# Capped attention and two feed-forward blocks: attention as one phase, two batches per pass over the weights

## The chip, the cores and the metric

The kernel runs on one core of a Trainium2 chip. The metric is the device time of one execution in microseconds. A core has TensorE (matmuls; PE, its weight loads PEld), VectorE (DVE), ScalarE (ACT), GpSimd (POOL) and SyncE (SP), whose queue issues all DMAs here.

## The reference

```python
# q, k, v: (4 batches, 12 heads, 448, 64) float32; weights arrive as float64
scores = cap * tanh(q @ k.T / 8 / cap)                  # per batch and head
attn = exp(scores - max); attn /= sum(attn)
x = (attn @ v), heads side by side                      # 1792 x 768
h = x @ w_in;  x = (h - tanh(h)) @ w_out                # 768 x 2048, 2048 x 768
h = x @ w_in2; out = (h * sigmoid(1.702 * h)) @ w_out2  # same sizes
```

## The kernel before

All activations lie with features on partitions and the 448 tokens of a batch as columns. A batch has six pairs of heads for attention, then four products (input and output of two layers), each 96 products of 128 x 128 weights by 448 columns.

**Attention of a pair** g: `prep` transposes q and k (TensorE) and copies them from PSUM; `pair_scores` makes scores for two of four key blocks; `tanh` and `exps` run on ScalarE over 112 x 896; `add` sums the exponentials on VectorE; `pair_pv` multiplies by v; `pair_sum` sums over keys with a matmul by ones; `pair_out` takes the reciprocal and the product. In the first batch (g < 6) this is float32 and runs alone, in an order written out by hand in `attention` (pinned by `pin`). The pairs of batches 1 to 3 are steps of a generator that the main loop at the end takes between feed-forward matmuls, at rates given by `ATT_RATES`; their scores are three float32r products of high and low halves.

**Weights** come in pieces ("chunks") of up to 6 x 128 x 128. `w_convert` makes float32 from the float64 words in four steps on ScalarE and VectorE (exponent, low bits, shift, or) and stores the result in DRAM (`kept`). Batch 0 uses the float32 piece as it is, with whole float32 matmuls. From batch 1 on `w_split` makes a float32r high half (`hi_act`, L95) and a low half (`lo_dve`, L101), for each batch anew, but for the first 16 pieces, whose halves are kept too. The products are then high x high, high x low, low x high.

**Between the products** `g_cubic` (layer one) makes h - tanh(h) with four ScalarE and four VectorE operations per 448 columns, L506 to L525; `g_gate` (layer two) takes one of each. From batch 1 on `g_split` adds a high half (ScalarE and VectorE in turn) and a low half on GpSimd (L104). The last product's columns are tokens; `final` transposes them back on TensorE ahead of the store.

**Order.** Tile's planner orders what is not pinned, by its own costs, within what buffers allow. `ahead` prepares pieces 4 (first batch) or 2 ahead; there are three buffers each for the double-width, float32 and half pieces.

Of the kernel before, what the change touches and what calls it, by code (L numbers as in the profile page):

```python
# [29 lines left out]
ATT_RATES = {"first": (0.0, 0.7, 0.7, 1.3), "last": (0.3, 1.1, 0.7, 1.1), "mid": (0.3, 0.9, 0.9, 0.8)}  # L30
ATT_END_0, ATT_END = 1.0, 0.97

LATE_AT = 8

LEAD_0 = 4
# [5 lines left out]
def attention_moe_moe(ctx, tc, q, k, v, cap, w_in1, w_out1, w_in2, w_out2, out):  # L41

# [9 lines left out]
    WCH = 6  # L66
# [6 lines left out]
    raw_p = pool("raw", 1)  # L73
    rv_p = pool("rawv", 2)
    st_p = pool("stk", 2)
    t_p = pool("t", 6)
    ts_p = pool("tsum", 2)
    w_p = pool("w", 2)
    big = pool("big", 1)
    g_p = pool("g", 2)  # L80
    g1_p = pool("g1", 1)
    wd_p = pool("wdbl", 3)
    wr_p = pool("wraw", 3)
# [3 lines left out]
    ps_b = pool("ps_b", 2, space=bass.MemoryType.PSUM)  # L87
# [12 lines left out]
    def lo_dve(dst, src, hi):  # L100
        nc.vector.tensor_tensor(out=dst, in0=src, in1=hi.bitcast(F32), op=ALU.subtract)  # L101

    def lo_pool(dst, src, hi):
        nc.gpsimd.tensor_tensor(out=dst, in0=src, in1=hi.bitcast(F32), op=ALU.subtract)  # L104
# [11 lines left out]
    xs_p = pool("xs", 2)  # L116
    xd = [dr_p.tile([P, S], F32, name=f"xd{i}") for i in range(NP)]
    xst = {}
    xf = [big.tile([P, S], F32, tag=f"xh{i}", name=f"xf{i}") for i in range(KM)]
    xh = [None] * KM  # L120
    xl = [big.tile([P, S], F32R, name=f"xl{i}") for i in range(KM)]

    first = ExitStack()
    t_f = first.enter_context(tc.tile_pool(name="t_f", bufs=4))
    wz_f = first.enter_context(tc.tile_pool(name="wz_f", bufs=1))
    raw_f = first.enter_context(tc.tile_pool(name="raw_f", bufs=2))
    ps_f = first.enter_context(tc.tile_pool(name="ps_f", bufs=2, space=bass.MemoryType.PSUM))
# [4 lines left out]
    for wi, wo in ((w_in1, w_out1), (w_in2, w_out2)):  # L132
        wi, wo = wi.bitcast(U32), wo.bitcast(U32)
        for f in range(KF):
            chunks.append((wi[:, 2 * f * P:2 * (f + 1) * P], 0, KM))
        for e in range(KM):
            for f0, f1 in parts:
                chunks.append((wo[:, 2 * e * P:2 * (e + 1) * P], f0, f1))
    NCH = len(chunks)
    split_kept = [i < KF for i in range(NCH)]  # L140
    kept_hl = [
        dr_p.tile([P, 2, k1 - k0, P], F32, name=f"kept_hl{i}") if split_kept[i] else None
        for i, (_, k0, k1) in enumerate(chunks)
    ]
    kept = [dr_p.tile([P, k1 - k0, P], F32, name=f"kept{i}") for i, (_, k0, k1) in enumerate(chunks)]
    dbls, raws, whl = {}, {}, {}
    gf, gh, gl = [None] * KF, [None] * KF, []
    n_dma, n_split, n_use = [0], [0], [0]

    n_dbl = [0]  # L150

    def dbl_dma():
        if n_dbl[0] < NCH:
            i = n_dbl[0]
            src, k0, k1 = chunks[i]
            t = wd_p.tile([P, WCH, P, 2], U32, tag="wd", name="wd")
            for a in range(k0, k1, WG):
                z = min(k1, a + WG)
                nc.sync.dma_start(
                    out=t[:, a - k0:z - k0].rearrange("p k f w -> p k (f w)"),  # L160
                    in_=src[a * P:z * P].rearrange("(k p) f -> p k f", p=P),
                )
            dbls[i] = t[:, :k1 - k0]
            n_dbl[0] += 1

    def w_dma(upto):
        while n_dma[0] <= min(upto, B * NCH - 1):
            i = n_dma[0]
            _, k0, k1 = chunks[i % NCH]
            if i >= 2 * NCH and split_kept[i % NCH]:  # L170
                h = wh_p.tile([P, WCH, P], F32R, tag="wh", name="wh")
                l = wh_p.tile([P, WCH, P], F32R, tag="wl", name="wl")
                for m, t in enumerate((h, l)):
                    nc.sync.dma_start(out=t[:, :k1 - k0].bitcast(F32), in_=kept_hl[i % NCH][:, m])
                whl[i] = (h, l)
            elif i >= NCH:
                t = wr_p.tile([P, WCH, P], F32, tag="wr", name="wr")
                nc.sync.dma_start(out=t[:, :k1 - k0], in_=kept[i % NCH])
                raws[i] = t
            n_dma[0] += 1  # L180

    def w_convert(i):
        _, k0, k1 = chunks[i]
        if i % 2:
            r = wh_p.tile([P, WCH, P], F32, tag="wh", name="wr")
        else:
            r = wr_p.tile([P, WCH, P], F32, tag="wr", name="wr")
        d = dbls.pop(i)
        high, half = d[:, :, :, 1], d.bitcast(U16)
        o = r[:, :k1 - k0]  # L190
        u = o.bitcast(U32)
        pin(nc.scalar.mul(out=o, in_=high.bitcast(F32), mul=2.0 ** -112))
        if i % 2:
            pin(nc.vector.tensor_scalar(
                out=half[:, :, :, 2], in0=half[:, :, :, 1], scalar1=F64_LOW, scalar2=None, op0=ALU.mult
            ))
        else:
            pin(nc.scalar.mul(out=half[:, :, :, 2], in_=half[:, :, :, 1], mul=F64_LOW))
        pin(nc.vector.tensor_scalar(out=u, in0=u, scalar1=3, scalar2=None, op0=ALU.logical_shift_left))
        pin(nc.vector.scalar_tensor_tensor(  # L200
            out=u, in0=high, scalar=0x80000007, in1=u, op0=ALU.bitwise_and, op1=ALU.bitwise_or
        ))
        dbl_dma()
        nc.sync.dma_start(out=kept[i], in_=r[:, :k1 - k0])
        return r

    def w_split(upto):
        while n_split[0] <= min(upto, B * NCH - 1):
            i = n_split[0]
            if i in whl:  # L210
                n_split[0] += 1
                continue
            _, k0, k1 = chunks[i % NCH]
            n = k1 - k0
            r = w_convert(i) if i < NCH else raws.pop(i)
            if i < NCH:
                whl[i] = (r, None)
                n_split[0] += 1
                continue
            h = wh_p.tile([P, WCH, P], F32R, tag="wh", name="wh")  # L220
            l = wh_p.tile([P, WCH, P], F32R, tag="wl", name="wl")
            hi_act(h[:, :n], r[:, :n])
            lo_dve(l[:, :n], r[:, :n], h[:, :n])
            if i // NCH == 1 and split_kept[i % NCH]:
                for m, t in enumerate((h, l)):
                    nc.sync.dma_start(out=kept_hl[i % NCH][:, m], in_=t[:, :n].bitcast(F32))
            whl[i] = (h, l)
            n_split[0] += 1

    def w_next():  # L230
        i = n_use[0]
        n_use[0] += 1
        w_split(i)
        return i, whl.pop(i)
# [4 lines left out]
    tt, sc_t, ts_t, r_t, sum_t = {}, {}, {}, {}, {}  # L239
    raw_done = set()  # L240
    last_raw = [None]

    def load_qk(g):
        if g >= NG or g in raw_done:
            return
        raw_done.add(g)
        b, hp = divmod(g, NP)
        t = (raw_f if g < NP and g % 3 else raw_p).tile([CP, 2, 2 * C * D], F32, tag="raw", name="raw")
# [8 lines left out]
    def load_v(g):  # L257
        if g >= NG or g in rawv:
            return
# [8 lines left out]
    def prep(g, i):  # L268
        t = raw[g]
        if i == 0:  # L270
            if g < NP:
                qkt[g] = st_p.tile([P, 2, S], F32, tag="ql", name="qk")
            else:
                qkt[g] = tuple(st_p.tile([P, 2, S], F32R, tag=tag, name=name) for tag, name in (("qh", "qk"), ("ql", "ql")))
        else:
            raw.pop(g)
        if 1 < g < NP:
# [5 lines left out]
        if g < NP:  # L283
            (hi_act if g == 0 and i else hi_dve)(qkt[g][:, i], ps[:, :S])
            return
        h, l = qkt[g]
        hi_act(h[:, i], ps[:, :S])
        lo_dve(l[:, i], ps[:, :S], h[:, i])

    def pair_kq(g, c):  # L290

        ps = ps_b.tile([CP, 2, 512], F32, tag="b", name="ps_sc")
        if g >= NP:
            h, l = qkt[g]
            seq = ((h, h), (h, l), (l, h))
        else:
            seq = ((qkt[g], qkt[g]),)
        for m, (qq, kk) in enumerate(seq):
            for j in range(2):
                a = slice(j * D, (j + 1) * D)  # L300
                pin(nc.tensor.matmul(  # L301
                    ps[:, j, :S], kk[a, 1, c * CP:(c + 1) * CP], qq[a, 0],
                    start=(m == 0), stop=(m == len(seq) - 1),
                ))
        sc_t[g, c] = ps

    def tanh(g, c):
        t = tt[g, c] = (t_f if g < NP and c % 2 else t_p).tile([CP, 2, S], F32, tag="t", name="t")
        pin(nc.scalar.activation(out=t, in_=sc_t.pop((g, c))[:, :, :S], func=AF.Tanh, scale=tsc[:CP]))  # L309

    def exps(g, c):

        t = tt[g, c]
        pin(nc.scalar.activation(out=t, in_=t, func=AF.Exp, scale=cpos[:CP]))  # L314
# [397 lines left out]
```

## Time and profile before

| | |
|---|---|
| three runs | 1227.54, 1227.92, 1228.9 us; median 1227.92 |
| profiled execution | 1227.54 us; its span 1225.8 us |
| TensorE busy | 1206.6 us, 98% |
| VectorE, ScalarE, GpSimd busy | 732.0, 696.7, 120.9 us |
| granted TensorE clock, mean | 0.997 |
| DMA | 202.86 MB, 165 GB/s in the mean |

The span runs from the first to the last instruction. Busy times are unions over an engine's instructions; a line such as L558 is a line of the kernel, and a helper's line (L95, L101) holds many uses of it.

### The profile page before, as it was taken

To read this page: it belongs to the slowest core of one execution; us is meant where nothing else is said; L and a number is where in the kernel's file an instruction comes from. 1 tells how busy PE (TensorE), PEld (TensorE's weight loads), DVE (VectorE), ACT (ScalarE), POOL (GpSimd) and SP (SyncE) were. 2 spreads that over 40 slices of the span, in tenths; PEclk is the share of its full clock that TensorE was granted. 3 is DMA by queue.
4 is the path that set the end of the run, shared out by engine and by line. 5 is a ranking of instruction groups with operands and counts; after the bars stand their busy time and mean duration, and the time that the engine had idled before them with its cause. 6 is when DMAs were issued, how large, how long until landed. Compare 5 with 4: busy or idle time off the path is not lost.

```text
span 1225.8 us, 15375 instructions
## 1 busy us (share of the span) xinstructions
PE 1206.6 (98%) x5535; PEld 895.7 (73%) x5535; DVE 732.0 (60%) x946; ACT 696.7 (57%) x953; POOL 120.9 (10%) x102
## 2 busy tenths in 40 slices
PE   9899999999999999999999999999999999999998
PEld 3245555545455788887788899887988799999997
DVE  5989845666554898455553589445455478534432
ACT  7889746566664677456654367556455467334421
POOL 0000000000000132002210033001310023103300
PEclk9999999999999999999999999999999999999999
DMA  8369887966765575343334575343443376333342
GB/s 205 108 219 313 278 259 240 294 216 216 240 196 164 207 271 163 113 120 96 115 107 141 166 211 152 104 120 115 114 123 115 106 225 175 109 119 107 96 126 57
DMA packets 163675, 202.86 MB, mean 165 GB/s; under 512 B 53264, under 2 KB 120592, under 8 KB 163600
## 3 DMA queue, kind: packets, MB, share of 16 engines
q1 hardware_dynamic: 163600, 201.89, 53.9%
q8 instruction: 43, 0.70, 0.2%
q14 instruction: 32, 0.26, 0.1%
HBM read 156.76 MB, written 45.09 MB: 165 GB/s over the span
## 4 chain that ended last, share of the span: by engine, by line
PE 88%; ACT 5%; DVE 4%; issue 1%; DMA 1%; SPq 0%; DVEq 0%; ACTq 0%
PE ps_y L582 39%; PE ps_h L558 39%; PE ps_sc L301 3%; PE ps_pv L332 3%; ACT t L309 2%; ACT t L314 2%; PE ps_r L345 1%; PE ps_qk L282 1%; DVE w L357 1%; PE ps_o L607 1%; DVE ts L324 1%; DMA raw<-in_k_dram 0%; DVE wl L101 0%; DVE ts L322 0%; PE wps L635 0%
## 5 line engine op out<-in xcount | busy, mean ns | idle before, releaser
L101 DVE TENSOR_TENSOR wl<-wr,wh 128x768 fp32r<-128x768 f32 (+1 forms) x172 | 159.9, 932 | 206.8 <-PE ps_y L582 88.0
L95 ACT CAST wh<-wr 128x768 fp32r<-128x768 f32 (+1 forms) x172 | 135.3, 788 | 210.8 <-PE ps_y L582 163.8
L558 PE MATMUL ps_h<-xh,wh 128*128 128x448 f32 x576 | 213.1, 370 | 3.9 <-DVE g_far L507 3.0
L582 PE MATMUL ps_y<-gl,wh 128*128 128x448 f32 x576 | 213.0, 370 | 0.0
L558 PE MATMUL ps_h<-xl,wh 128*128 128x448 f32 x576 | 212.2, 368 | 0.0
L582 PE MATMUL ps_y<-g,wh 128*128 128x448 f32 x576 | 210.9, 366 | 0.0
L582 PE MATMUL ps_y<-g,wr 128*128 128x448 f32 x384 | 148.1, 541 | 0.0
L558 PE MATMUL ps_h<-xf,wr 128*128 128x448 f32 x384 | 146.3, 540 | 0.5 <-DVE xf L353 0.5
L582 PE MATMUL ps_y<-g,wl 128*128 128x448 f32 x576 | 136.8, 367 | 0.0
L558 PE MATMUL ps_h<-xh,wl 128*128 128x448 f32 x576 | 133.8, 366 | 0.0
L104 POOL TENSOR_TENSOR gl<-g_q,g 128x448 fp32r<-128x448 f32 x48 | 63.4, 1321 | 702.8 <-ACT g L95 600.3
L558 PEld LDWEIGHTS ps_h<-xf,wr 128*128 128x128 f32 x384 | 72.2, 190 | 71.1 <-issue 69.3
L558 PEld LDWEIGHTS ps_h<-xh,wh 128*128 128x128 f32 x576 | 108.8, 189 | 15.9 <-DVE g_far L507 4.3
L582 PEld LDWEIGHTS ps_y<-g,wr 128*128 128x128 f32 x384 | 71.6, 190 | 66.7 <-issue 66.3
L309 ACT ACTIVATE t<-ps_sc,tsc 112x896 f32<-112x896 f32 x96 | 94.8, 1000 | 42.5 <-PE ps_sc L301 42.4
L558 PEld LDWEIGHTS ps_h<-xl,wh 128*128 128x128 f32 x576 | 108.9, 189 | 10.3 <-issue 0.8
L582 PEld LDWEIGHTS ps_y<-gl,wh 128*128 128x128 f32 x576 | 108.2, 188 | 11.0 <-issue 2.0
L582 PEld LDWEIGHTS ps_y<-g,wl 128*128 128x128 f32 x576 | 107.4, 188 | 10.7 <-issue 2.3
L558 PEld LDWEIGHTS ps_h<-xh,wl 128*128 128x128 f32 x576 | 108.0, 188 | 9.4 <-issue 0.3
L582 PEld LDWEIGHTS ps_y<-g,wh 128*128 128x128 f32 x576 | 108.3, 188 | 8.7 <-issue 0.3
L314 ACT ACTIVATE t<-t,cpos 112x896 f32<-112x896 f32 x96 | 98.8, 1043 | 1.9
L104 POOL TENSOR_TENSOR gl<-g_g,g 128x448 fp32r<-128x448 f32 x48 | 56.7, 1184 | 337.7 <-ACT g L95 247.5
(73 smaller groups left out, 1382.4 us busy)
## 6 DMA issues: line engine op xcount, KB each, us to landing
wr<-kept SPq DMA_DIRECT2D x100, 384.0 KB, 3.0
wd<-in_moe_w_in_dram SPq DMA_DIRECT2D x64, 384.0 KB, 4.8
wr<-kept SPq DMA_DIRECT2D x72, 320.0 KB, 2.9
wd<-in_moe_w_out_dram SPq DMA_DIRECT2D x48, 384.0 KB, 4.7
kept<-wr SPq DMA_DIRECT2D x44, 384.0 KB, 5.4
wh<-kept_hl SPq DMA_DIRECT2D x32, 384.0 KB, 3.4
wl<-kept_hl SPq DMA_DIRECT2D x32, 384.0 KB, 3.8
kept<-wr SPq DMA_DIRECT2D x24, 320.0 KB, 5.0
```

The lines of the kernel that those rows point to most:

```text
L95: pin(nc.scalar.copy(out=dst, in_=src))
L101: nc.vector.tensor_tensor(out=dst, in0=src, in1=hi.bitcast(F32), op=ALU.subtract)
L104: nc.gpsimd.tensor_tensor(out=dst, in0=src, in1=hi.bitcast(F32), op=ALU.subtract)
L282: pin(nc.tensor.transpose(ps[:, c * CP:(c + 1) * CP], t[:, i, c * P:(c + 1) * P], ident[:CP, :CP]))
L301: pin(nc.tensor.matmul(ps[:, j, :S], kk[a, 1, c * CP:(c + 1) * CP], qq[a, 0], start=(m == 0), stop=(m == len(seq) - 1),))
L309: pin(nc.scalar.activation(out=t, in_=sc_t.pop((g, c))[:, :, :S], func=AF.Tanh, scale=tsc[:CP]))
L314: pin(nc.scalar.activation(out=t, in_=t, func=AF.Exp, scale=cpos[:CP]))
L324: pin(nc.vector.tensor_tensor(out=ts_t[g], in0=ts_t[g], in1=t, op=ALU.add))
L332: pin(nc.tensor.matmul(r_t[g][j * D:(j + 1) * D, :S], rawv[g][:, j, kc, :], t[:, j], start=(kc == 0), stop=(kc == C - 1),))
L345: pin(nc.tensor.matmul(sum_t[g][j * D:(j + 1) * D, :S], ones[:CP], of[:, j], start=first, stop=last))
L558: pin(nc.tensor.matmul(ps[:, :S], w[:, kk, :], x[kk], start=(m == 0), stop=(m == len(seq) - 1)))
L582: nc.tensor.matmul(ps[:, :S], w[:, f - f0, :], x[f], start=(c == 0 and m == 0), stop=(c == len(parts) - 1 and m == len(seq) - 1),)
```

## The change

- Attention of all four batches is one phase ahead of the feed-forward, in the pinned order that only the first batch had, in float32 throughout. x of batches 0 and 1 is split into halves inside that phase (one tile in every second pair); x of batches 2 and 3 is stored to DRAM (`x_store`) and read back in the second pass (`x_next`). Two pieces of weights are converted and split in the phase, a step per pair.
- The feed-forward runs in two passes over the weights; each piece serves two batches in turn. All four batches use three float32r products. In the first pass every piece is converted, split and stored as halves (ScalarE: exponent, every other time the low bits, high half; VectorE: shift, or, low half, the low bits of the others); the second pass loads halves only. `LEAD` is 2; double-width and float32 pieces have two buffers, halves three.
- The low half of g is made on VectorE; g's high half on ScalarE.
- The last product has 128 tokens of the two batches as weights and 384 columns of w_out2 as moving operand, so that PSUM holds rows of tokens: seven banks at a time, twice per pass. `rows_out` scales them by 0.5 into one of two buffers and stores them in two DMAs; the transposes at the end are gone.
- PSUM in the feed-forward is eight single banks.

The diff, cut to its core:

```diff
+    wd_p = pool("wdbl", 2)
+    wr_p = pool("wraw", 2)
     wh_p = pool("whl", 3)
...
+            for half in range(2):
+                for f in range(0, KF, 2):
+                    chunks.append((wo[:, 2 * half * HW:2 * (half + 1) * HW], f, f + 2, HW))
...
+    def prepare(upto):
+        while n_ready[0] <= min(upto, NPASS * NCH - 1):
+            i = n_ready[0]
+            if i < NCH:
+                conv_exp(i)
+                conv_low(i, i % 2 == 0)
+                conv_shift(i)
+                conv_or(i)
+                conv_hi(i)
+                conv_lo(i)
+                continue
+            whl[i] = tuple(wh_p.tile([P, WC], F32R, tag=tag, name=tag) for tag in ("wh", "wl"))
+            n = width[i % NCH]
+            for m, t in enumerate(whl[i]):
+                nc.sync.dma_start(out=t[:, :n].bitcast(F32), in_=kept[i % NCH][:, m])
...
+        for g in range(NG):
             pair_act(g, 0)
+            if 2 <= g and g % 2 == 0:
+                x_split(*divmod(g // 2 - 1, NP), xs.pop(g // 2 - 1))
             pair_scores(g, 1)
             pair_act(g, 1)
+            load_v(g + 1)
...
             pair_pv(g, 0)
+            for c in range(1, C):
+                add(g, c)
+            for i in range(2):
+                prep(g + 2, i)
+            load_qk(g + 3)
+            if g == NG - 1:
+                hold[0] = True
+                for _ in range(15):
+                    next(moe_0)
+                hold[0] = False
             pair_scores(g + 1, 0)
             pair_pv(g, 1)
+            pair_sum(g)
             pair_out(g)
+            x_store(g)
+            for n, i in enumerate((NG - 9, NG - 5)):
+                for m, step in enumerate((conv_low, conv_shift, conv_or, conv_lo)):
+                    if g == i + m:
+                        step(n)
...
-        yield lo_pool(gl[f], g, gh[f])
+        yield hi_act(gh[f][:, s], g)
+        yield lo_dve(gl[f][:, s], g, gh[f][:, s])
...
+    def gemm_in(layer):
+        for f in range(KF):
+            i, (wh, wl) = w_next()
+            for s in range(NB):
+                ps = ps_next("ps_h")
...
+    def gemm_out_rows(b0):
+        blocks = NB * S // P
+        for half in range(2):
+            ps = [ps_next("ps_o") for _ in range(blocks)]
+            for j in range(KF // 2):
+                i, (wh, wl) = w_next()
+                for n in range(blocks):
+                    a = slice(n * P, (n + 1) * P)
+                    seq = [p for ff in range(2) for p in ((wh, gh, ff), (wl, gh, ff), (wh, gl, ff))]
+                    for m, (w, g, ff) in enumerate(seq):
+                        nc.tensor.matmul(
+                            ps[n][:, :HW], g[2 * j + ff].rearrange("p s n -> p (s n)")[:, a], w[:, ff, :],
...
+    def rows_out(b0, half, n, ps):
+        o = g_p.tile([P, S], F32, tag="q", name="o")[:, :HW]
...
+    attention()
+    pinned[0] = False
+    first.close()
+    ps_m = pool("ps_m", 6, space=bass.MemoryType.PSUM)
+    ahead(0)
+    for p in range(NPASS):
+        for _ in moe_0 if p == 0 else moe(p * NB):
+            pass
+        run_late()
```

## Rows read from the trace of the kernel before

**Rows 1.** The page's first part: busy us, share of the span, instructions

```profile
PE 1206.6 (98%) x5535; PEld 895.7 (73%) x5535; DVE 732.0 (60%) x946; ACT 696.7 (57%) x953; POOL 120.9 (10%) x102
```

**Rows 2.** Busy time of each engine in stretches, columns in the first line

```profile
core 0: us, PE busy (x) PEld busy (x) DVE busy (x) ACT busy (x) POOL busy (x), PEclk, DMA share, GB/s
19.50:28.11 8.61, 8.58 (x46) 3.21 (x48) 7.82 (x8) 7.83 (x9) 0.00 (x0) 1.00 0.99 307
...
70.00:142.00 72.00, 72.00 (x193) 36.34 (x192) 68.49 (x112) 62.15 (x90) 0.00 (x0) 1.00 0.91 299
...
1100.00:1200.00 100.00, 100.00 (x498) 92.08 (x497) 40.60 (x57) 38.36 (x57) 18.50 (x16) 1.00 0.38 112
```

**Rows 3.** The chain of waits, whole span: start us, us, engine, tile, line, count

```profile
66.35 70.95 PE ps_h L558 x188
...
983.39 57.93 PE ps_h L558 x284
1041.32 58.68 PE ps_y L582 x288
```

**Rows 4.** The timeline of attention: start us, us, engine, line, operation, [idle before]

```profile
19.50 2.96 DVE L352 RECIPROCAL w<-ps_r 128x448 f32<-128x448 f32 x1 [0.54 <-PE ps_r L345]
...
27.09 0.97 PE L345 MATMUL ps_r<-ts,ones 112*64 112x448 f32 x4
27.99 1.76 PE L301 MATMUL ps_sc<-qk 64*112 64x448 f32 x8
28.11 2.96 DVE L352 RECIPROCAL w<-ps_r 128x448 f32<-128x448 f32 x1 [0.54 <-PE ps_r L345]
...
31.34 0.98 PE L282 MATMUL ps_qk<-ident,raw 112*128 112x112 f32 x8
...
46.85 2.96 DVE L352 RECIPROCAL w<-ps_r 128x448 f32<-128x448 f32 x1 [0.54 <-PE ps_r L345]
```

**Rows 5.** VectorE's groups, 70 to 142 us (last row: whole span): busy us, mean ns

```profile
L200 DVE SCALAR_TENSOR_TENSOR wr<-wd,wr 128x768 uint32<-128x768 uint32 x16 | 15.2, 951 | 1.0 <-ACT wd L198 0.8
L525 DVE COPY_PREDICATED g<-g_m,g_far 128x448 f32<-128x448 uint16 x15 | 9.9, 663 | 0.9
L524 DVE SCALAR_TENSOR_TENSOR g<-g_q,g_t 128x448 f32<-128x448 f32 x16 | 9.9, 616 | 0.4
L518 DVE TENSOR_TENSOR g_t<-g_v,g_t 128x448 f32<-128x448 f32 x16 | 9.8, 615 | 0.4
L507 DVE TENSOR_TENSOR g_far<-ps_h,g_t 128x448 f32<-128x448 f32 x16 | 9.8, 612 | 0.0
L199 DVE TENSOR_SCALAR wr<-wr 128x768 uint32<-128x768 uint32 x15 | 8.6, 574 | 0.8 <-ACT wr L192 0.8
L194 DVE TENSOR_SCALAR wd<-wd 128x768 uint16<-128x768 uint16 x8 | 8.2, 1026 | 0.1
L200 DVE SCALAR_TENSOR_TENSOR wr<-wd,wr 128x640 uint32<-128x640 uint32 x4 | 3.3, 815 | 0.0
L199 DVE TENSOR_SCALAR wr<-wr 128x640 uint32<-128x640 uint32 x4 | 2.0, 500 | 0.0
L194 DVE TENSOR_SCALAR wd<-wd 128x640 uint16<-128x640 uint16 x2 | 1.7, 874 | 0.0
...
L101 DVE TENSOR_TENSOR wl<-wr,wh 128x768 fp32r<-128x768 f32 x100 | 97.8, 978 | 115.0 <-ACT wh L95 67.2 <-PE ps_h L558 25.4 <-PE ps_y L582 21.8
```

**Rows 6.** The timeline of weight loads: score matmuls of a later pair, transposes

```profile
22.72 0.78 PEld L282 LDWEIGHTS ps_qk<-ident,raw 112*128 112x128 f32 x8 [0.70 <-DVE w L352]
...
520.88 0.18 PEld L301 LDWEIGHTS ps_sc<-qk,ql 64*112 64x112 f32 x2
...
521.50 0.17 PEld L301 LDWEIGHTS ps_sc<-qk,ql 64*112 64x112 f32 x2
```

**Rows 7.** The end: timeline of TensorE; DMA issues of the output (median us to landing)

```profile
1218.33 1.17 PE L582 MATMUL ps_y<-g,wl 128*128 128x448 f32 x5
...
out_dram<-o SPq DMA_DIRECT2D x24, 224.0 KB, 2.9
```

More of the change, by code (lines that the diff above doesn't have):

```diff
@@ L26 @@
 F64_LOW = 0.936 * 2.0 ** -13
[L30 to L31 removed]
 LATE_AT = 8
[L35 removed]
+LEAD = 2
 WARM_UP = 11
@@ L159, in dbl_dma @@
                 nc.sync.dma_start(
-                    out=t[:, a - k0:z - k0].rearrange("p k f w -> p k (f w)"),
+                    out=t[:, (a - k0) * n:(z - k0) * n].rearrange("p (k f) w -> p k (f w)", f=n),
                     in_=src[a * P:z * P].rearrange("(k p) f -> p k f", p=P),
                 )
-            dbls[i] = t[:, :k1 - k0]
+            dbls[i] = t[:, :width[i]]
             n_dbl[0] += 1
[L166 to L180, printed above, removed]
@@ L205, in w_convert, with conv_hi @@
[L205 to L211, printed above, removed]
-                continue
[L213 to L228, printed above, removed]
+    def conv_hi(i):
+        whl[i] = tuple(wh_p.tile([P, WC], F32R, tag=tag, name=tag) for tag in ("wh", "wl"))
+        hi_act(whl[i][0][:, :width[i]], raws[i][:, :width[i]])
@@ L232, in w_next, with ahead @@
         n_use[0] += 1
-        w_split(i)
-        return i, whl.pop(i)
+        prepare(i)
+        n = chunks[i % NCH][3]
+        return i, tuple(t[:, :width[i % NCH]].rearrange("p (k f) -> p k f", f=n) for t in whl.pop(i))
+    hold = [False]
+    def ahead(i):
+        if not hold[0]:
+            prepare(i + LEAD)
     NG = B * NP
     raw, rawv, qkt = {}, {}, {}
-    tt, sc_t, ts_t, r_t, sum_t = {}, {}, {}, {}, {}
-    raw_done = set()
+    tt, sc_t, ts_t, r_t, sum_t, xs = {}, {}, {}, {}, {}, {}
     last_raw = [None]
     def load_qk(g):
-        if g >= NG or g in raw_done:
+        if g >= NG:
             return
-        raw_done.add(g)
         b, hp = divmod(g, NP)
-        t = (raw_f if g < NP and g % 3 else raw_p).tile([CP, 2, 2 * C * D], F32, tag="raw", name="raw")
+        t = raw_p.tile([CP, 2, 2 * C * D], F32, tag="raw", name="raw")
         for i, src in enumerate((q, k)):
@@ L335, in pair_pv, with pair_sum @@
                 ))
-    def pair_sum(g, of, first, last):
-        if first:
-            if g < NP:
-                sum_t[g] = ps_f.tile([P, 512], F32, tag="p", name="ps_r")
-            else:
-                sum_t[g] = ps_s.tile([P, 512], F32, tag="s", name="ps_r")
+    def pair_sum(g):
+        sum_t[g] = ps_f.tile([P, 512], F32, tag="p", name="ps_r")
         for j in range(2):
-            pin(nc.tensor.matmul(sum_t[g][j * D:(j + 1) * D, :S], ones[:CP], of[:, j], start=first, stop=last))
+            pin(nc.tensor.matmul(
+                sum_t[g][j * D:(j + 1) * D, :S], ones[:CP], ts_t[g][:, j], start=True, stop=True
+            ))
@@ L570, in gemm_out @@
-    def gemm_out(layer, b):
+            for s in range(NB):
+                ps = ps_next("ps_h")
+                seq = [p for kk in range(KM) for p in ((wh, xh[s], kk), (wh, xl[s], kk))]
+                seq += [(wl, xh[s], kk) for kk in range(KM)]
+                for m, (w, x, kk) in enumerate(seq):
+                    pin(nc.tensor.matmul(
+                        ps[:, :S], w[:, kk, :], x[kk], start=(m == 0), stop=(m == len(seq) - 1)
+                    ))
+                    if m == 0 and s == 0:
+                        ahead(i)
+                    if m == LATE_AT:
+                        run_late()
+                    if m < len(seq) - 1:
+                        yield
+                (g_cubic, g_gate)[layer](s, f, ps)
+                yield
@@ L588, in gemm_out @@
                         ahead(i)
-                    if m == LATE_AT // passes:
+                    if n == 2:
                         run_late()
-                    for _ in range(passes - (c == len(parts) - 1 and m == len(seq) - 1)):
-                        yield
-            if layer == 0 and b == 0:
-                (hi_dve if e % 2 else hi_act)(xf[e], ps[:, :S])
-            elif layer == 0:
-                hi_act(xh[e], ps[:, :S])
-                lo_dve(xl[e], ps[:, :S], xh[e])
-            else:
-                y = g_p.tile([P, S], F32, tag="q", name="y")
-                nc.scalar.mul(out=y, in_=ps[:, :S], mul=0.5)
-                late.append(lambda e=e, y=y: final(b, e, y))
```

466 lines of the change are left out of this document (160 added, 306 removed).

## Prediction

> **What bounds the kernel now.** First the page's line of busy times [rows 1]: TensorE is at work for 98% of the span, VectorE for 60%, ScalarE for 57%. A mean hides stages, so next the stretches [rows 2]. In the pair loop of the first batch TensorE is busy 8.58 of 8.61 us, VectorE and ScalarE 7.8 each. In the first product of the first batch (70 to 142 us) TensorE has no gap, but VectorE stands at 68.49 of 72 us. In the last batch TensorE alone is full (100 of 100 us) and the others are below half. The granted clock is 1.00, the 2.4 GHz level, in all of them. So TensorE's order of work is the time, and VectorE is the engine that can break it.
>
> The chain of waits gives TensorE's price per matmul [rows 3]. Batch 0 runs whole float32: 70.95 us for 188 instructions, 0.377 each, two instructions per product. Batches 1 to 3 run three float32r products of 0.204 each (57.93/284, 58.68/288).
>
> **Feed-forward on TensorE.** Before: batch 0 has 4 x 96 products of two instructions, 768 x 0.377 = 290 us; the other three 3 x 1152 x 0.204 = 705 us; together 995. After, all four batches take three float32r products. The input products of both layers are 2 x 2 x 576 = 2304 matmuls x 0.204 = 470.0; the output product of layer one 2 x 576 = 1152 x 0.2038 = 234.7. The last product becomes 14 blocks x 16 x 3 = 672 matmuls of 384 columns in a pass, 1344 in all, where 1152 of 448 would have stood: the same columns, more instructions. The trace has no float32r matmul of 384 columns. 448 columns at 2.4 GHz are 187 ns, so 17 ns come on top. If these belong to each instruction, one of 384 takes 160 + 17 = 177 ns and the product 237.5 us; if they grow with the columns, 175 and 235. The upper end is a bound by the weight load: one takes 92.08/497 = 0.185 us in the records [rows 2], and would hold the spacing at 0.185 to 0.204 (249 to 274 us). I take 177: score matmuls with 112 weight columns keep the same 0.204 spacing as those with 128 (520.88 to 521.50, three steps in 0.62) and eight loads of 128 columns pass in 0.78 us between the short transposes [rows 6]. Sum 942 us, some 53 less than before.
>
> The Trainium skill (TensorE: Matmul & The Clock Gate, "Back-to-back issue gap") gives a warm matmul N/2.4 plus 2.5 ns. The float32 instruction, two passes of 187, agrees with its 0.377 [rows 3]; the float32r one does not (0.204, not 0.189). By the rule the last product would cost 218 us, 19 less, which is rival (d) below. The skill's front page (Trainium Kernel Development and Optimization, "Performance Expectations") wants weight-load time rather than matmul time read as the bound: it is 92.08 of 100 us in the last batch [rows 2], and by that the narrower matmuls are the 0.185 to 0.204 case.
>
> **Attention as one phase.** Its 24 pairs run the order of the first batch's loop. The period there is 8.61 us, reciprocal to reciprocal (19.50, 28.11) [rows 4]. VectorE closes the loop: the copies of the next pair, 0.54 us of waiting for the row sum on TensorE, the reciprocal, the adds. Whatever is added to VectorE comes on top one for one: from 28.11 to 46.85 are two periods plus 1.52, and a shift (0.57) and an or (0.95) [rows 5] ran there. Added now: 11 low parts of x ahead of the last pair but one, 0.57 each with overlap, 6.3; of the two pieces of weights converted in this phase 2 x 3.5 less the last low part, 6.1; and the copies of a 25th pair are missing, -1.2. ScalarE, busy 7.83 of 8.61 us [rows 2], takes its x copies (one in two pairs) and four conversion steps into the 0.8 us that it has left; were that gone, they would add to the loop as VectorE's do, some 8 us in all. Reciprocal 22 starts at 19.5 + 22 x 8.61 + 6.3 + 6.1 - 1.2 = 220.1; the scores of pair 23 begin 0.1 ahead of it, and after scores and half the values product (27.99 to 31.34, 3.35) the first feed-forward matmul starts at 223.4. What is left of attention then, 2.6 us, and 942.2 would end TensorE at 1168.2 if nothing made it wait. Lower end of this part -4 (low parts hidden in the 0.54 wait), upper +18 (0.75 us per pair, three engines above 90% in one loop).
>
> The issue of attention's loads, of two early weight loads and of x stores is on the SP queue; per pair five loads and at most one store. The loads of the pair after next wait for a free raw buffer, now three, as they did. I cost it at nothing; the cover is that a pair is read two pairs ahead (17 us). Taken out from between the feed-forward matmuls of batches 0 to 2, attention leaves no hole there, since every matmul has its weights two pieces ahead.
>
> **First pass, layer one: VectorE.** Here the cover is gone. Before, batch 0 needed neither halves of weights nor of g. Now one piece of weights serves two batches, 36 x 0.204 = 7.34 us of TensorE, and VectorE has for each batch 0.612 + 0.615 + 0.616 + 0.663 and a low part like the second (0.615): 3.12, twice 6.24; and for the piece shift 0.574, or 0.951, low part 0.978 and every other time the low bits 1.026: 3.02. Together 9.26 in durations. Consecutive ones overlap: the ten groups of 70 to 142 us sum to 78.4 in 68.49 busy [rows 2, 5], a ratio of 1.145, so 8.1 us per piece if VectorE never waits, 8.5 at the 95% share it had there. That is above 7.34, so it sets the pace. VectorE comes free at about 232.6 (last reciprocal and product), the third piece is ready at 235.1, and the last g of 16 pieces at 235.1 + 16 x 8.5 = 371.1. TensorE, unstalled, has meanwhile run the two pieces of the next product that need only the first 11 g, and wants the last five at 226 + 17.8 x 7.34 = 356.7. The wait is 14.4 us. Bounds: 8.1 gives 8; no overlap and a chain in series gives 57 (below). The halves of g leave GpSimd, which nothing then waits for. The DMA engines carry 4 x 393 KB per piece in this pass (double-width weights in, both halves out), 214 GB/s at TensorE's pace, where 70 to 142 us carried 299 [rows 2]: hidden; if a load came late, it would hold the same conversions that already wait for VectorE. In the second pass VectorE has 6.24 of 7.34 and no conversion; in layer two 2 x 1.23 + 3.02; in the output products 3.0 of 6.1 or more: hidden.
>
> **Borders and tail.** I allow 2 us for the borders of stages. At the end blocks of 6 x 0.177 = 1.06 us finish faster than they leave: two buffers, each held for an eviction (0.6, like the 448-column rows) and a store (2.9) [rows 7]. The evictions start at 1.1, 2.1, 4.6, 5.6, 8.1, 9.1 and 11.6, the last store lands at 15.1 and the end is near 15.8, against TensorE's 7.4: a tail of 8.3, where it now is 6.3 (from 1218.33 + 1.17 to 1225.8). Without the held buffers 4, at worst 11.
>
> **Sum.** 1168.2 + 14.4 + 2 + 8.3 = 1192.9 of span. The profiled run has 1.7 us around its span (1227.54 against 1225.8) and lies 0.4 below the median. So 1195 us, 2.7% less.
>
> **Rivals.** (a) Weight load bounds the last product: 0.185 to 0.204 per matmul, +11 to +37, 1206 to 1232. For it: recorded loads of 0.185; against it the 112-column spacing. (b) Slower than before: the six conversion steps of a piece alternate between ScalarE and VectorE, and if the planner leaves them one behind the other, VectorE is held through them, about 5 us in the mean of even and odd pieces, plus 6.24: 11.2 a piece, a wait of 57 instead of 14, 1238. It decides from about 10.5 us a piece. For it: look-ahead falls from 4 to 2 pieces and raw buffers from 3 to 2. Against: at 70 to 142 us VectorE was kept 95% busy with both kinds of work mixed. (c) The attention loop stretches by 0.75 us a pair: 1213. For it: three engines at 7.8 to 8.6 of 8.61 us; against it: what was added there came one for one. (d) Float32r's extra 17 ns vanish at 384 columns: 1344 x 0.163 = 218 us, 1176. For it: the float32 instruction has no such extra; against it: at 448 columns every float32r matmul has it.
>
> **How the numbers follow.** Forecast 0.60; (a) 0.13, (b) 0.14, (c) 0.06, (d) 0.07. A measurement tells about 0.2% (2.5 us) from no change. Faster: forecast, (c), (d), most of (a), 0.81; the same 0.05, where (a) and (b) cross 1228; slower 0.14. Range 1180 to 1228, which leaves out (d) and most of (b).
>
> **What would show it.** In the profile after: reciprocals 8.6 to 9.2 us apart up to about 229; first feed-forward matmul at 223; VectorE above 93% and TensorE with gaps from about 265 to 380, and nowhere else; matmul spacing of 0.177 in the last product; a tail of 8. Wrong if the pieces of the first pass take 10.5 us or more, if the spacing is 0.19 or more, or if TensorE has gaps in the second pass.

## The result, and the profile after

The changed kernel takes 1190.22 us (median of four runs, 1188.65 to 1191.17); the kernel before, in the same series, 1228.41. The ratio is 0.9685, 95% interval 0.9669 to 0.9702: 3.1% faster, where 1195 us (2.7%) was forecast. The profiled execution has a span of 1188.2 us.

The page of the changed kernel, to be held against [rows 1]: busy us, share of the span, instructions.

```profile
PE 1159.9 (98%) x5867; PEld 962.1 (81%) x5867; DVE 662.5 (56%) x914; ACT 617.5 (52%) x870; POOL 0.7 (0%) x6
```

TensorE is busy 46.7 us less and still for 98% of the span: the bound is the same, its work is less. The chain of waits (start us, us, engine, tile, line, count) gives its price per matmul, as [rows 3] did:

```profile
376.05 97.55 PE ps_y L454 x480
473.60 116.74 PE ps_h L433 x576
...
707.90 119.03 PE ps_h L433 x576
...
945.97 119.04 PE ps_h L433 x576
1065.01 110.26 PE ps_o L477 x636
1176.19 1.89 DMA out_dram<-o
...
1181.98 2.02 DMA out_dram<-o
```

Divide us by count. 448 columns run at two spacings, 116.74/576 = 0.2027 and 119.03/576 = 0.2067 us, and each of these rows keeps one; 384 columns take 110.26/636 = 0.1733. The last rows are the tail: stores of the output, one waiting for the other. Busy time by stretch, for [rows 2]:

```profile
core 0: us, PE busy (x) PEld busy (x) DVE busy (x) ACT busy (x) POOL busy (x), PEclk, DMA share, GB/s
...
260.00:300.00 40.00, 40.00 (x195) 36.34 (x194) 38.53 (x66) 37.19 (x61) 0.00 (x0) 1.00 0.50 170
300.00:340.00 40.00, 40.00 (x196) 36.32 (x195) 38.60 (x65) 36.50 (x62) 0.00 (x0) 1.00 0.54 190
...
1060.00:1160.00 100.00, 100.00 (x574) 99.54 (x573) 4.30 (x8) 4.19 (x8) 0.00 (x0) 1.00 0.37 119
...
182.24:193.10 10.86, 10.86 (x50) 3.96 (x52) 10.04 (x11) 9.10 (x10) 0.00 (x0) 0.84 0.39 113
```

From 260 to 340 VectorE is at 96%, as forecast, but TensorE has no gap beside it. The groups of VectorE in these 80 us (busy us, mean ns), for [rows 5]:

```profile
L405 DVE COPY_PREDICATED g_q<-g_m,g_far 128x448 f32<-128x448 uint16 x20 | 13.5, 676 | 0.0
L77 DVE TENSOR_TENSOR gl<-g_q,gh 128x448 fp32r<-128x448 f32 x20 | 12.5, 625 | 0.8 <-ACT gh L71 0.7
...
```

Twenty of each, two per piece: ten pieces in 80 us, 8.0 us each. The timeline (start us, us, engine, line, operation, idle before it): VectorE's reciprocals, for [rows 4], and its last low half of g, then TensorE at the end of attention and of the first output tile, then ScalarE's evictions at the end, for [rows 7].

```profile
19.34 2.96 DVE L305 RECIPROCAL w<-ps_r 128x448 f32<-128x448 f32 x1 [0.54 <-PE ps_r L298]
...
27.95 2.96 DVE L305 RECIPROCAL w<-ps_r 128x448 f32<-128x448 f32 x1 [0.55 <-PE ps_r L298]
...
37.11 2.96 DVE L305 RECIPROCAL w<-ps_r 128x448 f32<-128x448 f32 x1 [0.54 <-PE ps_r L298]
...
152.77 2.96 DVE L305 RECIPROCAL w<-ps_r 128x448 f32<-128x448 f32 x1 [0.54 <-PE ps_r L298]
...
234.04 2.95 DVE L305 RECIPROCAL w<-ps_r 128x448 f32<-128x448 f32 x1
...
372.43 0.61 DVE L77 TENSOR_TENSOR gl<-g_q,gh 128x448 fp32r<-128x448 f32 x1
...
226.35 0.44 PE L433 MATMUL ps_h<-xh,wh 128*128 128x448 f32 x1 [0.46 <-DVE xs L307]
...
233.28 0.47 PE L433 MATMUL ps_h<-xh,wl 128*128 128x448 f32 x1
237.05 0.56 PE L433 MATMUL ps_h<-xh,wh 128*128 128x448 f32 x1 [3.29 <-DVE w L305]
237.40 0.58 PE L433 MATMUL ps_h<-xl,wh 128*128 128x448 f32 x1
...
362.57 0.47 PE L454 MATMUL ps_y<-gh,wh 128*128 128x448 f32 x1 [0.98 <-ACT wh L71]
...
369.44 0.47 PE L454 MATMUL ps_y<-gh,wh 128*128 128x448 f32 x1 [0.52 <-ACT wh L71]
...
374.40 0.36 PE L454 MATMUL ps_y<-gl,wh 128*128 128x448 f32 x1
...
376.05 0.47 PE L454 MATMUL ps_y<-gh,wh 128*128 128x448 f32 x1 [0.27 <-ACT wh L71]
...
1175.30 0.49 ACT L496 ACTIVATE o<-ps_o 128x384 f32<-128x384 f32 x1 [46.67 <-PE ps_o L477]
1178.24 0.49 ACT L496 ACTIVATE o<-ps_o 128x384 f32<-128x384 f32 x1 [2.45 <-DMA out_dram<-o]
```

The periods of the pair loop are 8.61 and 9.16 us in turn up to 152.77 (one is 9.03), and 9.1 to 11.5 behind it, where weights are converted too. The first feed-forward matmul starts at 226.35. At 233.28 TensorE stops, and 3.8 us pass to its next matmul: the PSUM bank of its next tile still holds the row sum of the last pair, which the reciprocal at 234.04 reads.

The waits of the first pass are 1.35, 0.89 and 0.63 us between matmul starts. By their rows all three are for the high half of a weight piece (`ACT wh`), none for g: the last low half of g is done at 373.04 and first read at 374.40. They end at 376.05, and from there TensorE runs on unbroken through two products. That row, the first matmul behind the third part, is what the expectations call the start of the third part, and the experiments the unbroken run. In the four kernels below whose edits lie behind it (columns, six buffers, nudges, float32) it stands at 375.42, 375.42, 376.23 and 377.30, so a microsecond there tells nothing.

### The profile page after: what moved, and what is told of

It is laid out like the page before. It is cut to its first block, busy times and chain, and to the rows that moved or that the text cites. A ratio compares the mean times of both kernels' runs of the same rounds, so it can differ in the third digit from the quotient of the medians.

```text
span 1188.2 us, 15381 instructions
## 1 busy us (share of the span) xinstructions
PE 1159.9 (98%) x5867; PEld 962.1 (81%) x5867; DVE 662.5 (56%) x914; ACT 617.5 (52%) x870; POOL 0.7 (0%) x6
## 4 chain that ended last, share of the span: by engine, by line
PE 74%; DVE 14%; ACT 5%; issue 3%; DMA 3%; SPq 0%; DVEq 0%; ACTq 0%
PE ps_h L433 30%; PE ps_y L454 18%; PE ps_o L477 18%; DVE w L305 3%; PE ps_sc L263 3%; DVE ts L282 3%; PE ps_pv L290 2%; PE ps_r L298 2%; DVE ts L280 1%; DMA out_dram<-o 1%; DVE wr L163 1%; DVE g_q L405 1%; PE ps_qk L253 1%; DMA wd<-in_moe_w_out_dram 1%; DVE wl L77 1%
## 5 line engine op out<-in xcount | busy, mean ns | idle before, releaser
L477 PE MATMUL ps_o<-wh,gh 128*128 128x384 f32 x448 | 149.9, 335 | 0.7 <-ACT o L496 0.7
L477 PE MATMUL ps_o<-wh,gl 128*128 128x384 f32 x448 | 149.7, 334 | 0.0
L477 PE MATMUL ps_o<-wl,gh 128*128 128x384 f32 x448 | 149.7, 334 | 0.0
L454 PE MATMUL ps_y<-gh,wh 128*128 128x448 f32 x384 | 141.1, 368 | 1.8 <-ACT wh L71 1.8
L77 DVE TENSOR_TENSOR wl<-wr,wh 128x768 fp32r<-128x768 f32 (+1 forms) x66 | 61.5, 932 | 54.2 <-ACT wh L71 28.5
L454 PE MATMUL ps_y<-gh,wl 128*128 128x448 f32 x384 | 90.3, 367 | 0.0
L263 PE MATMUL ps_sc<-qk 64*112 64x448 f32 x384 | 87.2, 574 | 0.6 <-ACT qk L71 0.6
L477 PEld LDWEIGHTS ps_o<-wh,gh 128*128 128x128 f32 x448 | 84.1, 188 | 1.2 <-ACT o L496 1.0
L477 PEld LDWEIGHTS ps_o<-wl,gh 128*128 128x128 f32 x448 | 84.1, 188 | 0.0
L477 PEld LDWEIGHTS ps_o<-wh,gl 128*128 128x128 f32 x448 | 84.1, 188 | 0.0
```

What stands on the lines that cost most here:

```text
L77: pin(nc.vector.tensor_tensor(out=dst, in0=src, in1=hi.bitcast(F32), op=ALU.subtract))
L263: pin(nc.tensor.matmul(ps[:, j, :S], qkt[g][a, 1, c * CP:(c + 1) * CP], qkt[g][a, 0], start=True, stop=True))
L454: nc.tensor.matmul(ps[s][:, :S], w[:, f - f0, :], x[f][:, s], start=(c == 0 and m == 0), stop=(c == len(parts) - 1 and m == len(seq) - 1),)
L477: nc.tensor.matmul(ps[n][:, :HW], g[2 * j + ff].rearrange("p s n -> p (s n)")[:, a], w[:, ff, :], start=(j == 0 and m == 0), stop=(j == KF ...
```

## The experiments

The theory: TensorE's feed-forward work fell by what float32 cost over three float32r products; VectorE paces attention and the first product, one for one. The rivals are named in each expectation.

**All low bits of the weights on VectorE** (more load on the suspected pacer):

```diff
-                conv_low(i, i % 2 == 0)
+                conv_low(i, False)
```

> The low bits of every piece of the first pass on VectorE, where the changed kernel has every other piece's on ScalarE. Theory (VectorE paces layer one of the first pass, 8.0 us a piece): 8 more operations of 1.03 us on VectorE in the stage, 0.82 to 0.94 each with overlap, so the third part of the next product starts 6.5 to 7.5 us later than 376.1 and the time is 1197 us. Rival (the stage is held by the chain of conversion steps or by the loads; VectorE has slack): ScalarE loses 1.92 us per even piece, the time stays at 1190 or falls, 1188 to 1191.

Measured: 1193.19 us (ratio to before 0.9714, 0.9694 to 0.9734). The unbroken run begins at 378.92 instead of 376.05, with five waits ahead of it instead of three, all for weight pieces. Load moved from ScalarE to VectorE does delay this product, but by 2.9 where 6.5 to 7.5 were expected. That ScalarE, at 91 to 93% there, was relieved by the same edit may be why; no run separates the two. In time the two intervals overlap.

**The first bank of the feed-forward is not the row sum's**:

```diff
+        if n_ps[0] % 8 in (7, 0):
+            return ps_n.tile([P, 512], F32, tag="n", name=name)
-    ps_m = pool("ps_m", 6, space=bass.MemoryType.PSUM)
+    ps_m = pool("ps_m", 4, space=bass.MemoryType.PSUM)
+    ps_n = pool("ps_n", 2, space=bass.MemoryType.PSUM)
```

> The first PSUM bank after the two of pool ps_s is taken from the place of the score banks, not of the row sum, so that TensorE need not wait for the last reciprocal. Theory (VectorE sets the end of the stage): the gap of 3.8 us at 233 goes, and comes back as longer waits at 361 to 376; third part at 375 to 376, time 1189 to 1190. Rival (TensorE's own path sets the end): the gap is a gain, 1187.

Measured: 1191.70 us (0.9707, 0.967 to 0.9744), no gain that the intervals show. TensorE's timeline:

```profile
232.80 0.36 PE L435 MATMUL ps_h<-xh,wh 128*128 128x448 f32 x1
...
343.89 0.74 PE L435 MATMUL ps_h<-xh,wh 128*128 128x448 f32 x1 [2.35 <-ACT wh L71]
```

The stop at 233 is gone, and a wait for weights at 341 is there instead; the unbroken run begins at 373.94, 2.1 earlier (1.5 to 3.4 against the kernels with an unchanged first pass). So of the gap of 3.8 a part came back inside the stage behind it, as theory wanted, and a part did not. The kernels with six buffers and with nudges have a wait like it at 343, without this edit: there the product ahead of it ran at the faster spacing, and TensorE came early in that way.

**The low halves of x on GpSimd during attention** (less load on VectorE):

```diff
-        lo_dve(xl[s][i], x, xh[s][i])
+        if pinned[0]:
+            pin(nc.gpsimd.tensor_tensor(out=xl[s][i], in0=x, in1=xh[s][i].bitcast(F32), op=ALU.subtract))
+        else:
+            lo_dve(xl[s][i], x, xh[s][i])
```

> The low halves of x in the attention phase on GpSimd. Theory (VectorE closes the loop of a pair): all reciprocals 8.6 us apart where no conversion runs, instead of 8.62 and 9.15 in turn; the stage behind starts and ends 6 us earlier, 1184. Rival (GpSimd's access slows VectorE as much as it relieves it, as at L524 of the kernel before, 0.96 beside GpSimd's work against 0.62 without): 1 to 2 us at most, 1188 to 1190.

Measured: 1184.59 us (0.9648, 0.9632 to 0.9664), 5.6 less. VectorE's timeline, and TensorE's first feed-forward matmul:

```profile
19.24 2.96 DVE L305 RECIPROCAL w<-ps_r 128x448 f32<-128x448 f32 x1 [0.54 <-PE ps_r L298]
...
27.86 2.96 DVE L305 RECIPROCAL w<-ps_r 128x448 f32<-128x448 f32 x1 [0.54 <-PE ps_r L298]
...
220.52 0.47 PE L436 MATMUL ps_h<-xh,wh 128*128 128x448 f32 x1
```

The first twelve periods are all 8.62 within 0.01, and the rest, most with conversions, 8.7 to 11.0; the 0.54 of each low half is gone, as theory wanted. Attention ends 5.8 earlier, and the gain stays to the end.

**No hoisted conversions**: `pinned[0] = False` moved behind `ahead(0)`, so that the steps of the third piece, which the planner had put into pairs 19 to 22, stay behind attention.

```diff
     attention()
-    pinned[0] = False
     ...
     ahead(0)
+    pinned[0] = False
```

> The first conversion behind the attention phase is pinned behind it, so that the planner can't take its steps into pairs 19 to 23. Theory (VectorE's work up to the third part is what counts, wherever it stands): attention ends some 3 to 4 us earlier, with less half clock, and the third part still starts at 375 to 377; time 1189 to 1191. Rival (the steps taken in cost more there than behind, since they stretch the loop of all engines and let the clock fall): 3 us gained, 1187.

Measured: 1193.87 us (0.9718, 0.9697 to 0.9738). The last reciprocal starts at 231.63, 2.4 earlier, but the unbroken run begins at 378.50, 2.4 later. The work taken out of the loop is done at 235 to 239, where VectorE is the pacer as well, and later than before. The rival's gain of 3 us did not come, nor did the run begin at 375 to 377, as theory had it.

**The last product by columns again**, with transposes ahead of the store (core of the edit):

```diff
-        if layer == 0:
+        if True:
...
-        gemm_out_rows(b0)
+        gemm_out(1, b0)
```

> The last product by columns again (576 matmuls of 448 a pass, weights as stationary), with transposes and one store per tile. Theory: 0.2027 to 0.2067 per matmul gives 233 to 238 us for both passes where the rows took 232.9 (1344 x 0.1733), and 24 transposed tiles at 0.55 us of TensorE give 13: some 16 us more, 1206. Rival (the narrower matmuls cost what the transposes did, or the transposes hide): within 3 us of 1190.

Measured: 1192.89 us (0.9723, 0.9695 to 0.975); the expected loss of 16 was missed. Its chain:

```profile
713.87 116.53 PE ps_h L434 x575
830.39 116.73 PE ps_y L455 x576
947.13 116.74 PE ps_h L434 x576
```

The last products with the transposes between their tiles do cost more, 122.6 and 120.9 us from first to last product matmul instead of 117.4 and 116.3: 10 together. But the three products behind the first of them run at 0.2027 instead of 0.2067 and give back 7. Rows of tokens are worth some 10 us on TensorE; the spacing of three products, which the edit was not meant to touch, is worth nearly as much.

**Six output buffers in the last pass**:

```diff
-        o = g_p.tile([P, S], F32, tag="q", name="o")[:, :HW]
+        o = g_p.tile([P, S], F32, tag=("q", "t", "far")[n // 2 % 3] if b0 + NB == B else "q", name="o")[:, :HW]
```

> Six output buffers in the last pass instead of two. Theory (the last evictions wait for stores two blocks back): evictions follow TensorE at 1.04 us, the last one at 1181.6 instead of 1184.2, 2.5 us gained, 1187.7. Rival (the queue that issues the 14 stores one by one, 9.6 us from first to last, sets the end anyway): less than 0.7 us gained.

Measured: 1189.80 us (0.9688, 0.9659 to 0.9718), within the spread. ScalarE's timeline:

```profile
1181.07 0.49 ACT L496 ACTIVATE o<-ps_o 128x384 f32<-128x384 f32 x1 [1.59 <-PE ps_o L477]
```

Evictions now wait for TensorE alone. The last matmul starts at 1180.64 and the span is 1185.4: 4.8 from there, instead of 7.0 (1181.16 to 1188.2).

**A short matmul of 16 to 136 columns ahead of each piece of the second pass**, into a bank that the piece then overwrites; in `gemm_in`, and alike at each tile in `gemm_out`:

```diff
+                if i >= NCH and s == 0:
+                    n = 16 + 8 * (i % 16)
+                    nc.tensor.matmul(ps[:, :n], wh[:, 0, :], xh[s][0][:, :n], start=True, stop=True)
```

> In the second pass one short matmul (16 to 136 columns, overwritten afterwards) ahead of each piece of the input products and each tile of the middle product. Theory (the spacing of a stream of matmuls locks to one of several values by the phase in which it starts: 0.2067 in the second pass, 0.2027 in the first, patterns of 0.204 in the kernel before): pieces show different spacings, and the 1728 matmuls take between 350 and 357 us plus 2 us for the short ones. Rival (0.2067 belongs to the second pass, its buffers or loads): all pieces stay at 0.2067, 2 us more.

Measured: 1191.59 us (0.9704, 0.9689 to 0.9718). TensorE's timeline, then two pieces of the chain:

```profile
721.31 0.18 PE L432 MATMUL ps_h<-xh,wh 128*128 128x40 f32 x1
721.34 0.45 PE L436 MATMUL ps_h<-xh,wh 128*128 128x448 f32 x1
721.63 0.37 PE L436 MATMUL ps_h<-xl,wh 128*128 128x448 f32 x1
721.83 0.36 PE L436 MATMUL ps_h<-xh,wh 128*128 128x448 f32 x1
...
788.18 7.35 PE ps_h L436 x36
795.59 7.35 PE ps_h L436 x36
```

Behind the short one the steps are 0.20, and a piece takes 7.41 us from start to start where 36 x 0.2067 are 7.44: the slow spacing goes, and the nudge itself costs about 0.11 (36 x 0.2027 = 7.30). One for each piece is too many. In the first pass, where no nudge stands, the middle product behind its last wait (99.46 us for 480 matmuls) and the layer-two input product (119.04 for 576) ran at 0.2067 here and not at 0.2027, which ate the rest.

**One of two batches of the second pass in whole float32** in three of the four products; its low halves are left out:

```diff
+                if i >= NCH and s == 0:
+                    seq = [(wh.bitcast(F32), [t.bitcast(F32) for t in xh[s]], kk) for kk in range(KM)]
```

> One of the two batches of the second pass takes whole float32 matmuls on the high halves in three of its four products (its low halves are left out of them). Theory (the change's gain is the price of float32 against three float32r products): per product 192 x 0.376 = 72.2 us instead of 288 x 0.2067 = 59.5, three times 12.7, so 38 us more, 1228. Rival (the gain comes from the order, not from the kind of matmul): under 10 us more.

Measured: 1225.5 us (0.9986, 0.9972 to 1.0001), all of the gain gone. The chain:

```profile
708.55 130.35 PE ps_h L435 x480
```

Each of the three products takes 11.3 us more, 34 together (38 expected: the other batch went to the 0.2027 spacing, 1.15 us a product). Taken by itself, float32 for one batch costs 12.4 us a product more than three float32r at 0.2067, and 13.6 more than at 0.2027; before, batch 0 paid it four times. The order was left as changed, so the rival, that the gain is the order's, is out.

**The three parts that had shown something, joined**: low halves of x on GpSimd, six output buffers, and one nudge of 32 columns at the first tile of each input and middle product.

```diff
+                if f == 0 and s == 0:
+                    nc.tensor.matmul(ps[:, :32], wh[:, 0, :], xh[0][0][:, :32], start=True, stop=True)
```

> The parts that gained, joined: x low halves of the attention phase on GpSimd, six output buffers in the last pass, and one short matmul (32 columns, overwritten) ahead of the first tile of each input and middle product. Theory: 5.6 (as in the run with GpSimd) + 2.3 (tail, as in the run with six buffers) + 3 x 2.2 (three products of the second pass at 0.2027 instead of 0.2067, 0.02 us a short matmul) = 14.5 us less than 1190.2, so 1176. Rival (the spacing falls back to 0.2067 within a product, or the tail's gain is taken up by the stores): 1180 or more.

Measured: 1176.65 us (0.9577, 0.9564 to 0.959), as expected. The chain:

```profile
369.38 99.46 PE ps_y L461 x480
...
703.76 116.83 PE ps_h L438 x576
...
937.45 116.82 PE ps_h L438 x576
1054.28 116.52 PE ps_o L484 x672
```

Three products at 0.2028, each 2.2 shorter than in the changed kernel, from one short instruction each. The rival came true in one place: the middle product of the first pass has a nudge at its head and runs at 0.2027 from there, but behind its last wait, from 369.38, at 0.2067 (99.46 us where the changed kernel has 97.55). That costs 1.9 of what was expected.

**The same with the bank order of the second experiment and a nudge ahead of each half of the last product**:

```diff
+                    if j == 0 and n == 0:
+                        nc.tensor.matmul(ps[0][:, :32], gh[0][:, 0, :P], wh[:, 0, :32], start=True, stop=True)
```

> The joined version with the PSUM order that lets the second batch's first tile start ahead of the last reciprocal, and with a short matmul ahead of each half of the last product too. Theory: the bank order gains 0 to 2 us, since VectorE sets the end of layer one; the spacing of the 384-column matmuls falls from 0.1733 towards 0.170 if it too is a lock, which would be 4 us in 1344: 1170 to 1176. Rival (0.1733 is the only spacing of this shape, the bank order gains nothing): 1176.

Measured: 1174.81 us (0.9571, 0.9555 to 0.9586), not told apart from the one before. The chain:

```profile
369.45 97.55 PE ps_y L463 x480
...
1051.94 58.37 PE ps_o L488 x336
```

A half of the last product takes 58.37 us for 336 matmuls, 0.1737 each with the nudge's own time: at 384 columns no faster spacing turned up. The unbroken run begins at 369.45 where the joined kernel's begins at 369.38, so the bank order gained nothing here. The 1.8 us between the two medians are the middle product, which by chance ran at 0.2027 behind its last wait this time.

**The joined kernel with the low half of g of the first of the two batches on GpSimd**, in layer one of the first pass:

```diff
-        yield lo_dve(gl[f][:, s], g, gh[f][:, s])
+        if n_use[0] <= KF and s == 0:
+            yield nc.gpsimd.tensor_tensor(out=gl[f][:, s], in0=g, in1=gh[f][:, s].bitcast(F32), op=ALU.subtract)
+        else:
+            yield lo_dve(gl[f][:, s], g, gh[f][:, s])
```

> The joined version with the low half of g of the first of the two batches on GpSimd in layer one of the first pass. Theory (VectorE's 8.0 us a piece set the end of that stage): 0.53 less a piece brings it to TensorE's 7.4, and the waits of some 3 us at the end of the stage go: 1172 to 1174. Rival (GpSimd's access stretches VectorE's two-input operations, 0.62 to 0.8 or more for about 1.2 us a piece, and the low half comes later): no gain or a loss, 1176 to 1182.

Measured: 1173.85 us (0.9563, 0.955 to 0.9576), the lowest median here and 1.4% below the changed kernel. The gain of 2.8 over the joined kernel is as forecast in size, but the intervals overlap, and it is not the forecast's gain. Groups from 260 to 340 us, then a row of TensorE's timeline:

```profile
L387 POOL TENSOR_TENSOR gl<-g_q,gh 128x448 fp32r<-128x448 f32 x10 | 28.1, 2814 | 54.9 <-ACT gh L71 54.9
...
L408 DVE TENSOR_TENSOR g_t<-g_v,g_t 128x448 f32<-128x448 f32 x19 | 13.7, 720 | 0.3 <-ACT g_v L404 0.3
...
363.72 0.47 PE L464 MATMUL ps_y<-gl,wh 128*128 128x448 f32 x1 [1.14 <-DVE gl L77]
```

In the joined kernel g_t took 625 ns. VectorE is spared 0.53 us a piece and loses about as much again: in 15 subtractions of GpSimd between 236 and 357 the one VectorE operation that each holds up takes some 0.5 us longer in the mean (last section). VectorE is not earlier: its last g_far starts at 361.22, in the joined kernel at 357.71, and here TensorE does wait for a low half of g. What the profiled executions differ by, 4.0 us, is 1.9 from the spacing of the middle product, as in the run before, and some 1.5 from the waits of the first pass, 5.0 together in the joined kernel and 3.5 here (one of 2.5 at 337 is absent). Why that one went is open.

## Why the prediction was right, and where its terms were off

The mechanism held: TensorE sets the time, and the gain is the price of float32. That the sum came within 5 us is in part luck, since it met by terms that cancel (us; gaps measured from matmul starts, less one spacing):

| step | forecast | measured | off by |
|---|---|---|---|
| first feed-forward matmul | 223.4 | 226.35 | +2.95 |
| feed-forward on TensorE | 942.2 | 943.3 | +1.1 |
| rest of attention inside it | 2.6 | 2.6 | 0 |
| handover at 231 to 241 | 0 | 6.0 | +6.0 |
| waits for VectorE, first pass | 14.4 | 2.3 | -12.1 |
| borders | 2 | 0.8 | -1.2 |
| tail | 8.3 | 6.85 | -1.45 |
| span | 1192.9 | 1188.2 | -4.7 |

**Feed-forward, right; two errors inside.** 704.7 us were forecast for the 448-column products at 0.204; they took 710.0, since four of six ran at 0.2067, the rest at 0.2027. The rows of tokens took 233.25 instead of 237.5 (0.1733, not 0.177). Against [rows 3], 995 to 943 is a gain of 52; the rest of the span grew from 231 to 245 us and gives 14 of it back. The float32 experiment shows where the 52 come from: four products at 12.4 to 13.6 are 50 to 54. The 14 are a difference; neither attention as one phase nor the two passes were undone by themselves.

**Rivals (a) and (d), both wrong.** The trace has weight loads busy for 99.54 of 100 us from 1060 to 1160, with a mean record of 0.188 us, while matmuls follow each other every 0.1733: the records overlap, and a load's record is not its price. Nor do the loads set the pace in another way: they are of 128 columns in both shapes, and yet the spacing falls by 29 ns or more from 448 to 384 columns. The Trainium skill (Trainium Kernel Development and Optimization, "Performance Expectations") calls MFU and the busy share of weight loads the good metrics of how close a kernel is to its roofline, and matmul busy time a bad one. It gives no price per matmul: read as one, as in rival (a), the load would have said 1206 or more. The extra of float32r at 384 columns is 13 ns, neither 17 nor none. By the Trainium skill (TensorE: Matmul & The Clock Gate, "Back-to-back issue gap") it is 2.5 ns: the trace has 13 at 384 columns and 16 or 20 at 448. The Trainium skill gives this rule there for an isolated matmul, and says that in a stream of weight loads and matmuls both set the spacing.

**Attention, +2.95.** The periods of 8.61 and 9.16 are those forecast (0.55 for each low half). The last eight periods took 81.3 us (152.77 to 234.04), where eight bare ones are 69: the two pieces' steps had been counted, the third piece's, which the planner hoisted in, had not. Without it (the experiment on hoisted conversions) the last reciprocal is 2.4 earlier, which is most of the 2.95. Twice in that stretch TensorE's granted clock fell to 1.2 GHz for a while (0.84 in the mean from 182.24 to 193.10), behind waits of 1.80 and 2.00 us for VectorE; behind a wait of 1.83 that ended at 221.57 it did not. Rival (c) did not come.

**Handover, missed.** The prediction did not ask which bank the first tile of the second batch takes. The bank-order experiment shows that it is a row sum's, and that its 3.8 us are worth less than that at the end: 2.1 there, nothing between the two joined kernels. The rest of the 6.0 is a wait of 0.5 for a row sum and matmuls at the 1.2 GHz level behind that stop (steps of 0.37 from 237.05, granted clock 0.53 up to 240.70).

**The step that failed: the wait of 14.4.** The prediction had TensorE wait for the last low half of g. VectorE's end was right: 8.0 us per piece (8.1 to 8.5 forecast) and that low half done at 373.0 (371.1 forecast). But TensorE never waited for it. Without its waits it would have come to the last five g (the row at 369.44) at 367.6, not 356.7: 3.0 later from attention, 6.0 from the handover, the rest from the slower spacing. And the wait had been counted to the start of that part, though the last g is used only near the end of its 30 matmuls, five us on (374.40). The 2.3 us of waiting that are left are of a kind that its sum had no term for: three pieces of weights whose high half, on ScalarE behind VectorE's shift and or, came late. So two of its signs did not show: TensorE has no gaps from 265 on, only from 361, and it stops at 233. Both engines' positions belong in such a term, not only the slower one's. Rival (b), conversions in series at 10.5 us or more a piece, is ruled out by the 8.0.

**Tail.** Held buffers, as forecast, but a store lands in 1.9 to 2.0 us there, not in the 2.9 that the median over all issues [rows 7] gave.

## What to carry to other kernels

When one engine paces a stage, other engines' delays ahead of it are paid out of its wait: add up arrival times on both sides before pricing a wait, read from the rows what each wait is for, and expect an edit ahead of it to come back at least in part as a wait inside it, unless it relieves the pacer itself. Price an instruction by the distance between starts in the stretch that bounds, not by its record or an engine's busy share. Before a difference of a few tenths of a per cent is put down to an edit, compare the spacing of the same instruction in the same stage of both kernels: twice here that was the whole difference or half of it.

## What the hardware showed that was not expected

- Float32r matmuls of 448 columns run at 0.2027 or 0.2067 us in the changed kernels, at the same full granted clock and with the same data flow; the kernel before has 0.204 besides [rows 3]. A stream mostly keeps its spacing up to an interruption and may leave that with another one: the middle product of the first pass ran at 0.2067 up to its wait at 361 and at 0.2027 behind it in the changed kernel, the other way round in the joined one (369.38). In the three joined kernels a single matmul of 32 columns at the head of a product was followed by 0.2027 in 17 of 18 cases, up to the next wait. Without one the choice changed with unrelated edits (columns instead of rows ahead of it: the faster; nudges in the other pass: the slower). What sets it is open; at 384 columns only 0.1733 to 0.1737 was seen.
- GpSimd's 128 x 448 subtraction took 1.13 us in attention (x, third experiment) and 2.81 beside layer one (g, last experiment). Two of those in the last experiment, each with the VectorE operation that it met last:

```profile
272.06 1.18 POOL L387 TENSOR_TENSOR gl<-g_q,gh 128x448 fp32r<-128x448 f32 x1 [5.08 <-ACT gh L71]
272.13 1.59 DVE L408 TENSOR_TENSOR g_t<-g_v,g_t 128x448 f32<-128x448 f32 x1
...
280.92 2.96 POOL L387 TENSOR_TENSOR gl<-g_q,gh 128x448 fp32r<-128x448 f32 x1 [7.69 <-ACT gh L71]
283.31 1.11 DVE L411 COPY_PREDICATED g_q<-g_m,g_far 128x448 f32<-128x448 uint16 x1
```

The first starts just ahead of a g_t and takes 1.18; the g_t, 0.62 elsewhere, takes 1.59. The second starts while VectorE is busy, lasts 2.96 beside five operations at their usual length, and only the predicated copy at its end, 0.68 elsewhere, is longer. The two look like turns taken and not like a shared rate. VectorE's own low half of g kept its 0.62 because it never met a GpSimd subtraction there. In the kernel before, from 400 us on the 21 operations of L524 that met one took 1.39 us in the mean and the 27 others 0.62; the 0.96 in the third expectation is the mean of both kinds. The Trainium skill (GPSIMD Engine Reference, "1. Specifications") says that GpSimd shares its SBUF interfaces with VectorE, with contention for instructions of two SBUF inputs or in a two-port mode; the g_t, with two inputs, agrees, and which mode the copy or the shift (1.52 instead of 0.57 at 338.32) runs in no run here shows.
